# A spectral and gated block with its gradients: inverse rows in a buffer of their own, activation-gradient matmuls dealt between filter chunks and inverse tiles, and the gate applied to w_down

## Chip, cores and metric

The kernel runs on one core of a Trainium2 chip. The metric is the device time in microseconds of one execution, as the median of several runs. Lower is better.

TensorE (PE in the profile, with its weight loads as PEld) does matmuls and writes to PSUM. ScalarE (ACT) and VectorE (DVE) copy results out of PSUM and do the elementwise work. GpSimd (POOL) and SyncE (SP) issue most DMAs; each takes its instructions in order, and so does every engine.

## What is computed

The reference is the forward pass of one block and, with `jax.vjp`, all its gradients. The sequence has S = 2048 positions, the width is D = 576, the hidden width is F = 4608, and everything is bfloat16 on the outside.

```python
def _A_ref(x, w_r, w_i):                       # spectral filter
    X = rfft2(x.astype(float32), axes=(-2, -1)) * (w_r + 1j * w_i)
    return irfft2(X, s=(S, D), axes=(-2, -1)).astype(bfloat16)
def _B_ref(x, w_gate, w_up, w_down):           # bilinear gated unit
    return ((x @ w_gate) * (x @ w_up)) @ w_down
...
sa, ca, ga, sb, cb, gb = split(silu(c) @ w_mod, 6)
h = layernorm(x) * (1 + ca) + sa
x = x + ga * _A_ref(h, w_r, w_i)
h = layernorm(x) * (1 + cb) + sb
x = x + gb * _B_ref(h, w_gate, w_up, w_down)
```

The outputs are the block's output and the gradients with respect to x, w_r, w_i, w_gate, w_up, w_down, c and w_mod, for a given `grad_out`. Two products of `grad_out` matter for this change. The gradient of the hidden activation is `(grad_out * gb) @ w_down.T`. The gradient of `w_down` is `hidden.T @ (grad_out * gb)`.

## The kernel before

The kernel has three parts: a head, a dense part over 36 blocks of 128 hidden columns, and a tail with the backward pass of the spectral filter. The change lies in the head, lines 187 to 477.

The 2048 positions are 16 tiles of 128 (`NT`). The two-dimensional transform is done by matmuls with tables of cosines and sines, in three stages.

- **Row transform** (`s1_norm`, `s1_cols`, `s1_rows`, L280 to L321). For each tile: layer norm and modulation into `hpp`, five transposes (`trp`, copied to `hT`), ten matmuls along the width (`zp`, copied to `zt`), and four along one factor of the sequence (`vp`, copied to `VA`). Statistics are taken for four tiles at once (`norm_stats`).
- **Filter chunks** (`s2_turn`, `s2_filter`, `s2_back`, `s2_inv`, L343 to L385). The 73 groups of four frequencies are handled in 19 chunks. A chunk is transposed from `VA` (`trv`, copied to `VT`), transformed (`xp`, copied to `Xc`), multiplied by the filter on VectorE (`fm`, then `Yg`), transposed back (`try_`, copied to `YT`) and inverse transformed (`ap_`). The last copy puts the result back into `VA`, over the chunk's own input, with the frequency as the outer index: neighbours in the copy's inner loop lie 32 elements apart.
- **Inverse tiles** (`s3_rows`, `s3_cols`, `s3_norm`, L395 to L446). For each tile, six matmuls from `VA` (`upa`, `upb`, copied to `ut`), twelve along the width (`yp`, copied to `yb`), and for each pair of tiles the residual, the second layer norm and its modulation into `h2p`, which a DMA transposes into `h2T`.

Each stage is software pipelined by `pipeline(n, steps)`, which in every round runs the later steps of earlier tiles first.

The six modulation vectors are made by `mod_make(j, wm)` from weights that `mod_load(j)` fetches into one of two `wm` buffers: ten matmuls (`modps`) and two copies to `modh[j]`, then a store to DRAM. The names are MSA, MCA, MGA for the first half and MSB, MCB, MGB for the second; MGB is the gate gb.

Then comes the **activation gradient** (L449 to L477). `grad_out` lies in `gon` and is multiplied in place by MGB, tile by tile (L452). Each tile is transposed on TensorE (L458, 80 matmuls) into `goT`. Blocks of `w_down` are loaded in pairs into `wdn2` and transposed by a DMA into `wdT`. For each of the 36 blocks there are four groups of five 512-column matmuls into `u4p` (L475), each copied out to `ghh_st`, on VectorE for the first nine blocks and on the two engines in turn after that. A finished block is stored to `ghhT_d` in DRAM, from which the dense part reads it. `ghh_st` has two buffers. The scaled `gon` is used again by the dense part, for the gradient of `w_down` (L526).

The program order is not the order on the engines. A planner sorts the instructions by priority, which falls along the program text, and by its own estimate of when each could run, so later instructions may be drawn forward into idle time. `tc.issue_after(i)` puts an instruction behind `i` on its engine, and `tc.high_priority` raises a priority. Once sorted, each engine and each DMA queue runs its list strictly in order, waiting on semaphores.

The dense part begins with matmuls into `gup` (L581). The tail holds the same spectral steps for the gradient. It keeps its inverse result in a buffer `j_A` of its own, laid out by part, row index and frequency (L835, written at L897, read at L924 and L925).

Of the kernel before, what the change touches and what calls it, by code (L numbers as in the profile page):

```python
# [9 lines left out]
FP32 = mybir.dt.float32  # L10
# [72 lines left out]
def build(ctx, tc, A_x, A_w_r, A_w_i, B_w_gate, B_w_up, B_w_down, c_in, w_mod, grad_out,  # L83
# [59 lines left out]
    def norm_stats(xt, pool, nt, name, rstd_out):  # L143

        st = pool.tile([128, nt, 2, nc.vector.BN_STATS_DIM], FP32, name=name + "_st")
        mv = pool.tile([128, nt, nc.vector.BN_AGGR_DIM], FP32, name=name + "_mv")
        for t in range(nt):
            for h in range(2):
                nc.vector.bn_stats(out=st[:, t, h, :], in_=xt[:, t, h * 288:(h + 1) * 288])
            nc.vector.bn_aggr(out=mv[:, t, :], in_=st[:, t, :, :])  # L150
        nc.scalar.activation(out=rstd_out, in_=mv[:, :, 1], func=ACT.Sqrt, bias=eps_t[:], scale=1.0)
        nc.vector.reciprocal(out=rstd_out, in_=rstd_out)
        nmr = pool.tile([128, nt], FP32, name=name + "_nmr")
        nc.vector.scalar_tensor_tensor(out=nmr[:], in0=mv[:, :, 0], scalar=-1.0, in1=rstd_out, op0=MUL, op1=MUL)
        return nmr
# [31 lines left out]
    with ExitStack() as hs:  # L187
# [17 lines left out]
        modh = [hp1.tile([128, D], BF, name="modh%d" % j) for j in range(6)]  # L205
# [9 lines left out]
        c_bf = hp1.tile([128, 5], BF, name="c_bf")  # L215
        nc.vector.memset(c_bf[:], 0.0)
        with nc.allow_non_contiguous_dma(reason="tiny c load"):
            nc.sync.dma_start(c_bf[:, 0:4], c_in[0, 0:512].rearrange("(m q) -> q m", q=128))
            nc.sync.dma_start(c_bf[64:128, 4:5], c_in[0, 512:576].rearrange("(m q) -> q m", q=64))
# [17 lines left out]
        def mod_load(j):  # L237
            wm = hw2.tile([128, 5, D], BF, name="wm")
            nc.sync.dma_start(wm[:, 0:4, :], w_mod[0:512, j * D:(j + 1) * D].rearrange("(m q) n -> q m n", q=128))
            nc.sync.dma_start(wm[:, 4, :], w_mod[448:576, j * D:(j + 1) * D])  # L240
            return wm

        def mod_make(j, wm):
            for h in range(2):
# [5 lines left out]
                else:  # L250
                    evac(modh[j][:, h * 288:(h + 1) * 288], ps[:, 0:288], eng="v")
# [4 lines left out]
        def x_load(c4):  # L256
            xt = hw2.tile([128, 4, D], BF, name="xt", bufs=3)
            nc.sync.dma_start(xt[:], x_v[:, 4 * c4:4 * c4 + 4, :])
            xts.append(xt)

        wms = {MSA: mod_load(MSA)}
        x_load(0)
        wms[MCA] = mod_load(MCA)
        T = {"RD": load_table(hp1, "RD", "tA")}
        T["G1"] = load_table(hp1, "G1", "tB")
        first = mod_make(MSA, wms[MSA])
        mod_make(MCA, wms[MCA])
        with tc.issue_after(first):
# [11 lines left out]
        def s1_norm(t):  # L280
            c4, tt = t // 4, t % 4
            if tt == 0:
# [4 lines left out]
                n1s["nmr"] = norm_stats(xts[c4], hw2, 4, "ln1", rstd1g[:, t:t + 4])  # L287
            n1 = n1s[c4]
            nc.scalar.activation(out=n1[:, tt, :], in_=xts[c4][:, tt, :], func=ACT.Identity, bias=n1s["nmr"][:, tt:tt + 1], scale=rstd1g[:, t:t + 1])
# [12 lines left out]
        def s1_cols(t):  # L302
            zt = zts[t] = hw2.tile([128, 2, FP], BF, name="zt", bufs=3)
            for cc in range(2):
# [3 lines left out]
                evac(zt[:, cc, :], zp[:, :FP], eng=("a" if cc == 0 else "v"))  # L308
            if t == 0:
                with tc.issue_after(mm.ins):  # L310
                    mod_make(MGB, wms[MGB])
# [14 lines left out]
        with tc.issue_after(first):  # L326
            nc.sync.dma_start(wn[:, 0, :, 0:DF], wr_v)
            nc.sync.dma_start(wn[:, 1, :, 0:DF], wi_v)
            for j in (MGA, MSB, MCB):
                wms[j] = mod_load(j)  # L330
        nc.gpsimd.dma_start(wn_d, wn[:].rearrange("k c a f -> k (c a f)"))
        for j in (MGA, MSB, MCB):
            mod_make(j, wms[j])
        r1.close()
        with ExitStack() as rc:
# [15 lines left out]
            def s2_filter(ci):  # L351
# [11 lines left out]
                Yg = Ygs[ci] = c2.tile([128, 4, 128], BF, name="Yg")  # L363
# [13 lines left out]
            def s2_inv(ci):  # L377
# [4 lines left out]
                Ac = VA[:, g0 * 128:(g0 + ng) * 128].rearrange("k (j f e) -> k j e f", f=4, e=2 * NT)  # L382
                evac(Ac, ap_[:, 0:ng, :].rearrange("k j (e f) -> k j e f", f=4), eng="a")

            pipeline(NCH, [s2_turn, s2_filter, s2_back, s2_inv])  # L385
# [6 lines left out]
        Av = VA[:].rearrange("k (f c a) -> k f c a", c=2, a=NT)  # L392
        uts, ybs = {}, {}

        def s3_rows(sa):  # L395
# [3 lines left out]
            for fc in range(3):  # L399
                f0 = FS[fc]  # L400
                o = upa[:, fc, :] if fc < 2 else upb[:, 0, :]
                nc.tensor.matmul(o, lhsT=Av[:, f0:f0 + 128, 0, sa], rhs=T["GB"][:, sa, 1:3, :].rearrange("k v s -> k (v s)"), start=True, stop=False)
                nc.tensor.matmul(o, lhsT=Av[:, f0:f0 + 128, 1, sa], rhs=T["GB"][:, sa, 0:2, :].rearrange("k v s -> k (v s)"), start=False, stop=True)
# [17 lines left out]
        def s3_norm(sa):  # L421
# [14 lines left out]
            for i in range(2):  # L436
# [3 lines left out]
                nc.vector.tensor_tensor(out=h2p[:, s0 + i, 0:D], in0=nm[:], in1=modh[MSB][:], op=ADD)  # L440
# [5 lines left out]
        pipeline(NT, [s3_rows, s3_cols, s3_norm])  # L446


        goT = u4.tile([128, NT, 5, 128], BF, name="goT")  # L449
        for t in range(NT + 1):  # L450
            if t < NT:
                nc.vector.tensor_tensor(out=gon[:, t, :], in0=gon[:, t, :], in1=modh[MGB][:], op=MUL)  # L452
            t -= 1
            if t < 0:
                continue
            pt = u4ps.tile([128, 5, 128], BF, name="u4p")
            for m in range(5):
                nc.tensor.transpose(pt[:, m, :], gonf[:, t * D + m * 128:t * D + (m + 1) * 128], ident[:])  # L458
            evac(goT[:, t, :, :], pt[:])
        FB4 = 2  # L460
        turns = []
        for fb0 in range(0, NFB, FB4):
            wdT = u4w.tile([128, FB4, 5, 128], BF, name="wdT")
            wdn = wdn2[:, (fb0 // FB4) % 2, :, :]
            with tc.issue_after(first):
                nc.sync.dma_start(wdn[:, :, 0:D], B_w_down[fb0 * 128:(fb0 + FB4) * 128, :].rearrange("(j f) d -> f j d", f=128))
# [661 lines left out]
```

## Time and profile before

| quantity | value |
|---|---|
| median of 3 runs | 1629.16 us (1628.55 to 1631.51) |
| the profiled execution's time | 1636.95 us |
| its span, first to last instruction | 1635.2 us |
| TensorE busy | 1566.0 us (96%) |
| VectorE busy | 1007.8 us (62%) |
| ScalarE busy | 567.6 us (35%) |
| mean granted TensorE clock | 0.987 |
| bytes moved by DMA | 280.35 MB |

"Busy" counts an engine as busy while an instruction is in progress. Matmuls overlap in the array, so a TensorE that shows 96% is not at its peak all that time. How many matmuls start in a stretch says more. A row of the groups view gives source line, engine, operation, output and inputs, shapes and count, then busy time and mean duration in ns, then the idle time of the engine just before, with what ended it. An `x` row on line 139 or 141 is a copy out of PSUM by a helper; the tile's name says which one.

### The profile page before, as it was taken

The page shows a single profiled execution, that of the slowest core. Times are in us where ns is not written, and L with a number is a line of the kernel's source. Part 1 is how long each engine was busy: PE and PEld are TensorE (multiplying, and loading weights), DVE is VectorE, ACT ScalarE, POOL GpSimd, SP SyncE. Part 2 cuts the span into 40 slices and gives each one's busy share as a digit, 9 for nine tenths or more (in the row PEclk, how much of TensorE's full clock was granted, in tenths as well). Part 3 has the DMA queues.
Part 4 walks back from the last instruction along what each step waited for, and adds up shares of the span by engine and source line. Part 5 has one row for each costly group of instructions (what it writes and reads, how often), then busy time and mean ns, then how long its engine had stood idle before and what let it go on. Part 6 is the DMA issues. An engine that isn't in the chain of part 4 may idle for free.

```text
span 1635.2 us, 29989 instructions
## 1 busy us (share of the span) xinstructions
PE 1566.0 (96%) x11354; PEld 1066.1 (65%) x11354; DVE 1007.8 (62%) x2642; ACT 567.6 (35%) x1056; POOL 161.3 (10%) x266
## 2 busy tenths in 40 slices
PE   6999999999999999999999999999999879899997
PEld 4645544566767676666767676666766656677765
DVE  7878733566564747565564747565564764678645
ACT  5697522322222222222222222222222355565022
POOL 0101100101000010101010010101000001100232
PEclk9999999999999999999999999999999989999998
DMA  9866976586768586776767686876757786636674
GB/s 349 289 183 196 267 214 192 148 162 123 145 134 165 114 170 121 158 147 114 161 129 153 135 161 117 161 135 142 158 103 136 190 240 202 231 97 193 254 216 151
DMA packets 482242, 280.35 MB, mean 171 GB/s; under 512 B 404753, under 2 KB 449426, under 8 KB 481202
## 3 DMA queue, kind: packets, MB, share of 16 engines
q1 hardware_dynamic: 462098, 204.26, 55.1%
q0 software_dynamic: 20000, 74.19, 15.5%
q8 instruction: 88, 1.44, 0.4%
q14 instruction: 56, 0.46, 0.1%
HBM read 108.51 MB, written 82.31 MB: 117 GB/s over the span
## 4 chain that ended last, share of the span: by engine, by line
PE 74%; DMA 6%; DVE 4%; issue 2%; ACT 2%; SPq 0%; POOL 0%; ACTq 0%; DVEq 0%; POOLq 0%
PE u57p L526 25%; PE gup L581 19%; PE u8p L607 17%; PE u4p L475 6%; PE u3p L1028 3%; DMA Xn<-xn_d 2%; DMA n2c<-n_d 2%; DMA wdB<-in_B_w_down_dram 1%; PE yp L937 1%; DMA out_dram<-o 1%; PE zp L801 1%; DVE gwt L849 0%; ACT u L956 0%; DMA x1t<-x_d 0%; DVE fm L167 0%
## 5 line engine op out<-in xcount | busy, mean ns | idle before, releaser
L612 DVE TENSOR_TENSOR acc<-acc,u8p 128x288 f32<-128x288 f32 x1088 | 429.4, 450 | 352.5 <-PE u8p L607 351.2
L581 PE MATMUL gup<-h2T,wgu 128*128 128x512 bf16 x1440 | 433.1, 379 | 0.0
L607 PE MATMUL u8p<-wT,ggT 128*128 128x288 bf16 x1152 | 314.7, 286 | 4.4 <-DVE acc L612 4.4
L607 PE MATMUL u8p<-wT,guT 128*128 128x288 bf16 x1152 | 314.7, 286 | 0.0
L581 PEld LDWEIGHTS <-wgu 128*128 128x128 bf16 x1440 | 140.8, 98 | 96.7
L528 ACT CAST so<-u57p 128x288 bf16<-128x288 f32 x216 | 86.2, 399 | 326.9 <-PE u57p L526 325.0
L607 PEld LDWEIGHTS <-guT 128*128 128x128 bf16 x1152 | 112.8, 98 | 101.5 <-issue 4.8
L475 PE MATMUL u4p<-goT,wdT 128*128 128x512 bf16 x720 | 165.0, 379 | 1.4 <-ACT ghh_st L139 1.4
L582 ACT CAST gT<-gup 128x512 bf16<-128x512 f32 x144 | 84.4, 586 | 226.6 <-PE gup L581 226.6
L526 PE MATMUL u57p<-gon,hh_sf 128*128 128x288 bf16 x1152 | 150.0, 287 | 0.0
L582 ACT CAST uT<-gup 128x512 bf16<-128x512 f32 x144 | 84.4, 586 | 188.5 <-PE gup L581 186.7
L526 PE MATMUL u57p<-h2p,gu_sf 128*128 128x288 bf16 x1152 | 148.8, 286 | 0.0
L526 PE MATMUL u57p<-h2p,gg_sf 128*128 128x288 bf16 x1152 | 148.2, 286 | 0.0
L1028 PEld LDWEIGHTS <-hl 128*128 128x128 bf16 x1152 | 112.9, 99 | 41.0 <-issue 11.3
L526 PEld LDWEIGHTS <-hh_sf 128*128 128x128 bf16 x1152 | 113.1, 98 | 35.1
L607 PEld LDWEIGHTS <-ggT 128*128 128x128 bf16 x1152 | 112.9, 98 | 29.0
L526 PEld LDWEIGHTS <-gu_sf 128*128 128x128 bf16 x1152 | 112.7, 98 | 28.4
L526 PEld LDWEIGHTS <-gg_sf 128*128 128x128 bf16 x1152 | 112.5, 98 | 28.3
L475 PEld LDWEIGHTS <-wdT 128*128 128x128 bf16 x720 | 69.2, 98 | 74.7 <-issue 1.9
L141 DVE CAST ghh_st<-u4p 128x512 bf16<-128x512 f32 x90 | 61.8, 687 | 67.7 <-PE u4p L475 64.7
L1028 PE MATMUL u3p<-wdB,hl 128*128 128x288 bf16 x672 | 96.4, 291 | 6.6 <-DMA wdB<-in_B_w_down_dram 5.8
L586 POOL DMA_DIRECT2D hhT_d<-hhT x36 | 33.2, 922 | 602.4 <-DVE hhT L583 598.7
(355 smaller groups left out, 1682.6 us busy)
## 6 DMA issues: line engine op xcount, KB each, us to landing
ghhT_d<-ghh_st SPq DMA_DIRECT2D x36, 512.0 KB, 3.3
ghh<-ghhT_d POOLq DMA_DIRECT2D x36, 512.0 KB, 7.7
hhT_d<-hhT POOLq DMA_DIRECT2D x36, 512.0 KB, 6.6
hl<-hhT_d SPq DMA_DIRECT2D x32, 576.0 KB, 7.9
out_dram<-woT SPq DMA_DIRECT2D x72, 128.0 KB, 2.0
wdn<-in_B_w_down_dram SPq DMA_DIRECT2D x18, 288.0 KB, 3.4
out_dram<-so SPq DMA_DIRECT2D x36, 144.0 KB, 2.4
wgu<-in_B_w_up_dram POOLq DMA_DIRECT2D x18, 256.0 KB, 5.3
```

The costliest lines, as they stand in the source:

```text
L141: nc.vector.tensor_copy(dst, src)
L475: nc.tensor.matmul(pt[:], lhsT=wdT[:, j, m, :], rhs=goT[:, 4 * sb4:4 * sb4 + 4, m, :], start=(m == 0), stop=(m == 4))
L526: mm = nc.tensor.matmul(pw[:, 0:288], lhsT=sf[:, t, :], rhs=rhs_n[:, t, h * 288:(h + 1) * 288], start=(t == 0), stop=(t == NT - 1))
L528: nc.scalar.copy(so[:, h * 288:(h + 1) * 288], pw[:, 0:288])
L581: nc.tensor.matmul(pt[:], lhsT=wgu[:, wi_, m, jw * 128:(jw + 1) * 128], rhs=h2T[:, ts_, m, :], start=(m == 0), stop=(m == 4))
L582: nc.scalar.copy(dstT[:, ts_, :], pt[:])
L586: nc.gpsimd.dma_start(hhT_d[:, :, fb, :].rearrange("tp f x -> f tp x"), hhT[:].rearrange("f (tp ti) p -> f tp (ti p)", ti=2))
L607: nc.tensor.matmul(pu[:, 0:288], lhsT=l_, rhs=r_, start=(k == 0), stop=(k == len(mms) - 1))
L612: nc.vector.tensor_tensor(out=dst, in0=dst, in1=pu[:, 0:288], op=ADD)
L801: nc.tensor.matmul(zp[:, :FP], lhsT=gyTs[t][:, m, :], rhs=T["RD"][:, m, cc, :], start=(m == 0), stop=(m == 4))
L937: nc.tensor.matmul(yp[:, 0:288], lhsT=ut[:, fc, cc * 128:(cc + 1) * 128], rhs=T["IR"][:, fc, cc, h * 288:(h + 1) * 288], start=(k == 0), s ...
L1028: mm = nc.tensor.matmul(p2[:, 0:288], lhsT=hls[fb // 9][:, fb % 9, ti * 128:(ti + 1) * 128], rhs=(wdA[:, fb] if fb < 15 else wdB[:, fb - 1 ...
```

## The change

The inverse copy of the filter chunks writes a new buffer `A_h`, laid out as the tail's, and the inverse tiles read their weights from it. The activation-gradient loop becomes a function `u4_group(g)` that does one group of five matmuls. Four groups are issued after the modulation, two in every round of the chunks' pipeline, two after every inverse tile's row matmuls (copied out by ScalarE), and the rest after the tiles. The chunks' pipeline becomes one step longer and `Yg` gets a third buffer.

The gate is applied to the pairs of `w_down` blocks after their load, ahead of the transpose, so `goT` is transposed from the unscaled `gon`; `gon` itself is still scaled, after the last inverse tile's `h2p`. `modh[MGB]` moves to another pool.

At the start, `c` is fetched with a higher priority. The first tile of x is loaded by itself, then MCA's weights, then the other three tiles, then MSA's weights. MCA is made before MSA, whose copies go to ScalarE. The first tile's statistics are taken alone, those of the next three together. MGB is made after the third tile rather than the first, with its copies on ScalarE. In odd tiles both `zt` copies are on ScalarE. MCB's weights are loaded by GpSimd's queue.

```diff
-    def norm_stats(xt, pool, nt, name, rstd_out):
+    def norm_stats(xt, pool, nt, name, rstd_out, room=None):
...
-        modh = [hp1.tile([128, D], BF, name="modh%d" % j) for j in range(6)]
+        modh = [(u4 if j == MGB else hp1).tile([128, D], BF, name="modh%d" % j) for j in range(6)]
...
+        with tc.high_priority(60), nc.allow_non_contiguous_dma(reason="tiny c load"):
+            c_bf = hp1.tile([128, 5], BF, name="c_bf")
...
         def x_load(c4):
             xt = hw2.tile([128, 4, D], BF, name="xt", bufs=3)
-            nc.sync.dma_start(xt[:], x_v[:, 4 * c4:4 * c4 + 4, :])
             xts.append(xt)
-        wms = {MSA: mod_load(MSA)}
+            t0 = 1 if c4 == 0 else 0
+            if t0:
+                nc.sync.dma_start(xt[:, 0:1, :], x_v[:, 0:1, :])
+                wms[MCA] = mod_load(MCA)
+            nc.sync.dma_start(xt[:, t0:4, :], x_v[:, 4 * c4 + t0:4 * c4 + 4, :])
+        wms = {}
         x_load(0)
-        wms[MCA] = mod_load(MCA)
+        wms[MSA] = mod_load(MSA)
...
-        first = mod_make(MSA, wms[MSA])
         mod_make(MCA, wms[MCA])
+        first = mod_make(MSA, wms[MSA], "a")
...
-                n1s["nmr"] = norm_stats(xts[c4], hw2, 4, "ln1", rstd1g[:, t:t + 4])
+            if t == 0 or tt == (1 if c4 == 0 else 0):
+                n = 1 if t == 0 else 4 - tt
+                nmr = norm_stats(xts[c4][:, tt:tt + n, :], hw2, n, "ln1", rstd1g[:, t:t + n], 4)
+                for k in range(n):
+                    n1s["nmr", t + k] = nmr[:, k:k + 1]
...
-                evac(zt[:, cc, :], zp[:, :FP], eng=("a" if cc == 0 else "v"))
-            if t == 0:
+                evac(zt[:, cc, :], zp[:, :FP], eng=("a" if cc == 0 or t % 2 else "v"))
+            if t == 2:
                 with tc.issue_after(mm.ins):
-                    mod_make(MGB, wms[MGB])
+                    mod_make(MGB, wms[MGB], "a")
...
-            for j in (MGA, MSB, MCB):
+            for j in (MGA, MSB):
                 wms[j] = mod_load(j)
         nc.gpsimd.dma_start(wn_d, wn[:].rearrange("k c a f -> k (c a f)"))
+        wms[MCB] = mod_load(MCB, nc.gpsimd)
         for j in (MGA, MSB, MCB):
             mod_make(j, wms[j])
+        goT = u4.tile([128, NT, 5, 128], BF, name="goT")
+        for t in range(NT):
+            pt = u4ps.tile([128, 5, 128], BF, name="u4p")
+            for m in range(5):
+                nc.tensor.transpose(pt[:, m, :], gonf[:, t * D + m * 128:t * D + (m + 1) * 128], ident[:])
+            evac(goT[:, t, :, :], pt[:])
+        FB4 = 2
+        turns, wdTs, sts, u4_done = [], {}, {}, [0]
+        def u4_group(g, eng=None):
+            fb, sb4 = g // 4, g % 4
+            k, j = fb // FB4, fb % FB4
+            if g % (4 * FB4) == 0:
+                wdTs[k] = u4w.tile([128, FB4, 5, 128], BF, name="wdT")
+                wdn = wdn2[:, k % 2, :, :]
+                with tc.issue_after(first):
+                    nc.sync.dma_start(wdn[:, :, 0:D], B_w_down[fb * 128:(fb + FB4) * 128, :].rearrange("(j f) d -> f j d", f=128))
+                nc.vector.tensor_tensor(out=wdn[:, :, 0:D], in0=wdn[:, :, 0:D], in1=modh[MGB][:].unsqueeze(1).to_broadcast([128, FB4, D]), op=MUL)
+                turns.append(nc.sync.dma_start_transpose(out=wdTs[k][:].rearrange("q j m f -> q (j m) f"), in_=wdn.rearrange("f j d -> f (j d)")).ins)
+            if sb4 == 0:
+                sts[fb] = u4w.tile([128, NT, 128], BF, name="ghh_st", bufs=2)
+            pt = u4ps.tile([128, 4, 128], FP32, name="u4p")
+            for m in range(5):
+                nc.tensor.matmul(pt[:], lhsT=wdTs[k][:, j, m, :], rhs=goT[:, 4 * sb4:4 * sb4 + 4, m, :], start=(m == 0), stop=(m == 4))
+            evac(sts[fb][:, 4 * sb4:4 * sb4 + 4, :], pt[:], eng=eng)
+            if sb4 == 3:
+                nc.sync.dma_start(ghhT_d[fb * 128:(fb + 1) * 128, :], sts[fb][:].rearrange("f t p -> f (t p)"))
+        def u4_groups(n, eng=None):
+            for _ in range(n):
+                u4_group(u4_done[0], eng)
+                u4_done[0] += 1
+        u4_groups(4)
         r1.close()
+        A_h = pool("hA", 1).tile([128, 2, NT, FP], BF, name="A_h")
...
-                Yg = Ygs[ci] = c2.tile([128, 4, 128], BF, name="Yg")
+                Yg = Ygs[ci] = c2.tile([128, 4, 128], BF, name="Yg", bufs=3)
...
-                Ac = VA[:, g0 * 128:(g0 + ng) * 128].rearrange("k (j f e) -> k j e f", f=4, e=2 * NT)
+                Ac = A_h[:].rearrange("k c a f -> k (c a) f")[:, :, f0:f0 + w].rearrange("k e (j f) -> k j e f", f=4)
...
-            pipeline(NCH, [s2_turn, s2_filter, s2_back, s2_inv])
+            pipeline(NCH, [s2_turn, s2_filter, lambda ci: u4_groups(2), s2_back, s2_inv])
...
-                nc.tensor.matmul(o, lhsT=Av[:, f0:f0 + 128, 0, sa], rhs=T["GB"][:, sa, 1:3, :].rearrange("k v s -> k (v s)"), start=True, stop=False)
+                nc.tensor.matmul(o, lhsT=A_h[:, 0, sa, f0:f0 + 128], rhs=T["GB"][:, sa, 1:3, :].rearrange("k v s -> k (v s)"), start=True, stop=False)
...
-        pipeline(NT, [s3_rows, s3_cols, s3_norm])
-        goT = u4.tile([128, NT, 5, 128], BF, name="goT")
...
+        pipeline(NT, [lambda sa: (s3_rows(sa), u4_groups(2, "a")), s3_cols, s3_norm])
+        u4_groups(4 * NFB - u4_done[0])
+        with tc.issue_after(h2_made[-1]):
+            for t in range(NT):
                 nc.vector.tensor_tensor(out=gon[:, t, :], in0=gon[:, t, :], in1=modh[MGB][:], op=MUL)
```

The old loop over the pairs of `w_down` blocks (L462 to L477) is removed; its loads, transposes, matmuls, copies and stores are those of `u4_group`, without the scaling.

## The prediction

> **What bounds the kernel now.** I read the whole span first in stretches cut where the head's stages change on TensorE: the row transform ends at 63.7 us, filter chunks run 71.2 to 132.5, inverse tiles 132.5 to 186.5, then activation-gradient matmuls alone (`u4p`, L475) until the first `gup` matmul at 293.5. Columns: stretch, its length, busy time (instructions) of PE, PEld, DVE, ACT and POOL, granted clock, DMA share, GB/s.
>
> ```profile
> 0.00:63.70 63.70, 48.48 (x388) 33.36 (x389) 51.32 (x165) 39.71 (x75) 5.14 (x16) 0.95 0.93 318
> 71.20:132.50 61.30, 56.00 (x461) 30.31 (x459) 48.60 (x131) 57.81 (x56) 5.16 (x9) 1.00 0.64 198
> 132.50:186.50 54.00, 49.96 (x351) 34.09 (x351) 45.90 (x136) 35.84 (x74) 10.81 (x20) 1.00 0.82 230
> 186.50:293.50 107.00, 105.65 (x490) 47.74 (x489) 38.73 (x66) 31.94 (x55) 2.47 (x5) 1.00 0.75 213
> 293.50:1635.20 1341.70, 1299.30 (x9611) 915.69 (x9609) 819.10 (x2139) 399.89 (x794) 137.71 (x216) 0.99 0.69 157
> ```
>
> The chunks are bound by ScalarE (57.81 of 61.30), the tiles by no engine alone, everything from 186.5 by TensorE. The last row matters most: the diff leaves 293.5 onwards alone, so what the head saves is saved whole. The chain of waits confirms it: the 107 us before `gup` are matmuls back to back, broken once by a store that must land before its buffer is refilled.
>
> ```profile
> 189.62 0.61 DVE ghh_st L141
> ...
> 190.29 5.58 DMA ghhT_d<-ghh_st
> ...
> 196.61 8.81 PE u4p L475 x40
> ...
> 206.12 87.57 PE u4p L475 x405
> 293.70 8.63 PE gup L581 x40
> ```
>
> Next, groups of instructions by line: why the chunks wait for ScalarE.
>
> ```profile
> L139 ACT CAST VA<-ap__1175 128x512 bf16<-128x512 f32 x1 | 2.5, 2537 | 0.0
> L139 ACT CAST Xc<-xp 128x512 bf16<-128x512 f32 x18 | 14.3, 792 | 2.5 <-PE xp L355 2.5
> L139 ACT COPY VT<-trv 128x512 bf16<-128x512 bf16 x18 | 12.2, 677 | 2.9 <-PE trv L347 2.9
> L897 ACT CAST j_A<-apt 128x512 bf16<-128x512 f32 (+1 forms) x19 | 11.1, 583 | 0.4 <-PE apt L896 0.4
> ```
>
> The inverse copy into `VA` takes 2.54 us, its siblings of equal size 0.6 to 0.8. `VA` steps 32 elements between neighbours of the inner loop. The backward pass (L897) makes the same copy into the layout that `A_h` will have, in 0.58 us. In the timeline the `VA` copies start at 92.8, 96.0, 99.2, 102.4: 3.2 us a chunk.
>
> **TensorE's work, counted.** A u4 group is five 512-column matmuls and one copy out, 144 groups in all. In the chain, 87.4 us from 206.12 to the first `gup` at 293.5 hold 82 groups (some records are missing), 1.066 us each. The stretch from 186.5 then holds about 99; the tiles, by 62 weight loads of L475, 12.4; the chunks about 32. A chunk's own 16 small matmuls start four in 0.22 us: 0.88 us. A tile's own are 6 row matmuls 0.11 apart and 12 column matmuls in 1.46 (the 12 `yp` last 1.64, less one pipeline tail): 2.1 us. So TensorE is unused for 61.3 - 19 x 0.88 - 32 x 1.066 = 10.5 us in the chunks and 54 - 16 x 2.1 - 12.4 x 1.066 = 7.2 us in the tiles, then about 1.5 us, and 0.9 us at 69 us, where it waits for the MCB weights: 20 us can be won there, by filling holes.
>
> **The change, part by part.**
>
> *Own buffer.* 18 full copies go from 2.54 to 0.58 us: 35 us of ScalarE in a stage of 61. A chunk then needs on ScalarE 0.6 + 0.7 + 0.6, plus one of its two group copies at 0.59: 2.5 us. VectorE: products 0.76, sums 0.49, `YT` 0.41, the other group copy 0.68, a quarter of a w_down scaling 0.2: 2.55. TensorE: 0.88 + 2 x 1.066 = 3.01. TensorE becomes the bound. Weight loads of `VA`, 143 ns, become 98 as at L924; their matmuls already start 0.11 apart, so I count nothing (at most 96 x 0.045 = 4 us if those loads set the pace).
>
> *Groups dealt out.* 4 groups before the chunks, 2 per chunk (38), 2 per tile (32), 70 left. A tile costs 2.1 + 2.13 = 4.23 us of TensorE; ScalarE 0.6 + 0.8 + 0.86 + 0.15 + 2 x 0.59 = 3.6; VectorE (45.9 us busy per 16 tiles, less 8 group copies of 0.67, plus 4 scalings) 2.8. I take 3.15 a chunk and 4.35 a tile, 3 to 5% over the sum, since in-order engines meet imperfectly, and 2.5 us a stage for filling and draining. The ends: exact sums with 1.5 us a stage; or 3.4 and 4.7 if ScalarE's copies queue behind each other.
>
> *Gate scales w_down.* 18 new VectorE products of 128x1152. No row has that form; the 128x576 ones take 0.45 alone and start 0.37 apart, so 0.8 us, 14.4 in all (bounds 0.45 and 0.90). The 16 `gon` products (0.45) leave the row transform, where VectorE is above 9.8 of 10 us from 30 to 60, and follow the last tile, where it is busy 38.73 of 107: nothing on the path. Were that cover gone, the hidden 7.2 us would show at the first `hh_sf` product near 316. The scaling is one more link, load, VectorE, transpose, on a chain of 3.4 + 3.4 us per pair of filter blocks; pairs are needed every 8 groups, 8.5 us, from two buffers. Nothing, unless VectorE waits for the load (a rival below).
>
> *Row transform.* Today the first tile waits for four tiles' statistics (square root at 12.98) and its transposes start at 15.62; the MGB matmuls stand between, so the second transposes come at 22.29. After it both are 2.5 to 2.7 us apart, set by transposes, copy `hT`, column matmuls in turn.
>
> ```profile
> 15.62 0.71 PE L298 MATMUL trp<-ident,hpp 128*128 128x128 bf16 x5 [3.86 <-DVE hpp L293]
> 17.49 2.62 PE L307 MATMUL zp<-T_RD,hT 128*128 128x292 bf16 x10 [1.15 <-ACT hT L139]
> 19.89 2.58 PE L247 MATMUL modps<-wm,sc_rep 128*128 128x288 bf16 x10
> 22.29 0.46 PE L298 MATMUL trp<-ident,hpp 128*128 128x128 bf16 x5
> ```
>
> With `c` issued ahead of the weights (0.5 us), one tile loaded and measured alone, and MCA made first, MSA's evacuation on ScalarE ends near 12.9 and the first transposes start near 13.4: 2.2 us earlier. The second follow at about 17.7, 4.6 earlier. MGB's ten matmuls (1.3 us warm) return after tile 2, half of them in the step's 0.5 us hole: -0.6. Three more small statistics operations (0.5) and eight zt copies moved to ScalarE lie beside this. I take 4 us, between 0 (the row transform is 0.93 full of DMA, and loads behind the first store issue 1 us later) and 7. The Trainium skill, "TensorE: Matmul & The Clock Gate", Part 1, says that an idle window of about 3.4 us halves TensorE's clock. The trace agrees: ten column matmuls take 2.62 us here at a granted 0.77, and 1.42 at 61.40. By that rule the thinner early work could stay slow one step longer and leave 3 us of the 4.
>
> *MCB's load on POOL's queue.* Its buffer is free only once MGA's matmuls are done, as now, but it no longer stands ahead of SP's table loads; on POOL it is behind the `wn_d` store, issued at 40.8. A 256 KB load lands in 5.1 us from POOL and 3.1 from SP in the list of DMA issues, so 2 us later; transposes and the four groups cover it. The Trainium skill, "DMA: Bandwidth & Descriptors", Specifications, gives 1 us against 0.6 for the first byte; by that the delay is 0.4 us.
>
> **Sum.** Row transform ends 63.7 - 4 = 59.7. Modulation 30 x 0.122 = 3.7, 38 transposes 2.1, four groups 4.3, wait 0.7: 10.8. Chunks 19 x 3.15 + 2.5 = 62.4. Tiles 16 x 4.35 + 2.5 = 72.1. Rest 70 x 1.066 + 1 = 75.6. `gup` starts at 280.6 instead of 293.5: 12.9 us less, span 1622.3. That execution took 1636.95 us in all, 7.8 over the runs' median of 1629.16; I take the saving off the median: 1616.
>
> **Rivals.**
>
> (a) *No holes*: 3.01, 4.23, 1.5 us of filling each, and 4 us won early: 6.6 us more, 1609. For: 105.65 of 107 today with nothing beside. Against: chunks and tiles have four stages with latencies.
>
> (b) *Copies bind the tiles*: ScalarE, 3.6 us of work a tile, must take group copies in order with `ut`, for which column matmuls already wait 10 us in all. At 5 us a tile, 10.4 of the gain goes: 1627.
>
> (c) *VectorE stuck on w_down, slower*: today SP bears the wait for that load (SP's waits: us in all, times, longest).
>
> ```profile
> SPq L477 <- DVE ghh_st L141: 28.1, 12, 5.4
> ...
> SPq L467 <- DMA wdn<-in_B_w_down_dram: 8.6, 2, 5.2
> ```
>
> After it, VectorE does, in order, with the chunk's products behind it and TensorE behind them; SP's store of `ghh_st`, which already waits 28.1 us for copies, comes late behind the transpose too. Held 1.2 us in each of 17 pairs, that is 20 us: 1637. It decides from 12.9 / 17 = 0.76 us a pair. Against: 16 of 18 transposes found their load landed.
>
> (d) *It doesn't do what it says*: the order on TensorE comes from a planner that already drew 44 groups forward, and may deal them as before: about 1629 if the copies' time then falls to no one.
>
> **How the numbers follow.** Forecast 0.60, with its own range 1607 to 1624; (a) 0.12, (b) 0.12, (c) 0.13, (d) 0.03. 0.2%, about what a measurement of this kernel can tell from no change, is 3.3 us: faster takes the forecast, (a) and over half of (b), 0.78; the rest of (b) and (d) make 0.08 for no change; slower 0.14. From 1605 to 1631 leaves out (c) and a little below.
>
> **What would show it.** `A_h` copies near 0.6 us; chunks 3.0 to 3.3 us apart with ScalarE no longer full; tiles 4.2 to 4.6 apart; about 70 groups after the last tile; first transposes before 14 us; `gup` near 281. Chunks at 3.5 or more, or VectorE idle before the scaling on a DMA, make it wrong.

## The result, and the profile after

The changed kernel takes 1642.67 us (median of 4 runs, 1641.52 to 1646.16), beside 1629.72 us for the kernel before. The ratio is 1.0082, with a 95% interval of 1.0063 to 1.0101: it is slower by some 13 us, where 13 us less were forecast.

First the stretches of the span, cut at the same events as before: end of the row transform, first chunk, first inverse tile, end of the tiles, first `gup`. Columns as before: stretch, length, busy time of PE, PEld, DVE, ACT and POOL, granted clock, DMA share, GB/s.

```profile
0.00:69.90 69.90, 50.34 (x415) 36.11 (x416) 46.33 (x146) 47.17 (x92) 5.13 (x16) 0.93 0.85 290
69.90:86.10 16.20, 10.35 (x52) 5.57 (x51) 3.95 (x9) 1.58 (x3) 1.31 (x2) 0.79 0.65 227
86.10:145.50 59.40, 58.87 (x488) 35.19 (x487) 42.95 (x119) 39.98 (x75) 0.52 (x1) 1.00 0.59 179
145.50:219.00 73.50, 68.97 (x447) 42.94 (x446) 49.82 (x137) 49.94 (x101) 13.95 (x26) 1.00 0.84 236
219.00:305.60 86.60, 78.66 (x350) 34.70 (x349) 36.80 (x67) 22.47 (x39) 3.96 (x8) 0.94 0.73 210
305.60:1640.80 1335.20, 1296.21 (x9604) 914.88 (x9609) 819.41 (x2139) 399.79 (x794) 137.54 (x216) 0.99 0.70 157
```

Set against the working of the prediction, the row transform ends at 69.9 us instead of 59.7, the modulation stretch lasts 16.2 instead of 10.8, the chunks 59.4 instead of 62.4, the tiles 73.5 instead of 72.1 and the rest 86.6 instead of 75.6. The sum is `gup` at 305.6 instead of 280.6. The chunks are what they were meant to be, with TensorE busy for 58.87 of 59.40. The loss lies in the row transform, the modulation and the rest, and the low clocks (0.93, 0.79, 0.94) stand in just these rows.

The copy that was 2.54 us, from the timeline of the same run (start, length, engine, line, operation):

```profile
93.34 0.60 ACT L139 CAST A_h<-ap__1180 128x512 bf16<-128x512 f32 x1
```

Next the waits: engine and line, what it waited for, us in total, times, longest.

```profile
DVE wdn L360 <- DMA wdn<-in_B_w_down_dram: 41.4, 15, 8.7
...
PE modps L247 <- DMA wm<-in_w_mod_dram: 6.2, 2, 5.8
```

The first line is rival (c), and larger than it was priced: VectorE stands 41.4 us before the scaling of `w_down`, where (c) took 20. The timeline shows where the large ones end on TensorE. The bracket at the end of a line is the idle time before the instruction, and what ended it.

```profile
59.70 0.76 DVE L360 TENSOR_TENSOR wdn<-wdn,modh 128x1152 bf16<-128x1152 bf16 x1 [5.09 <-DMA wdn<-in_B_w_down_dram]
60.89 0.28 PE L326 MATMUL vp<-zt,T_G 128*128 128x292 bf16 x1 [4.22 <-DVE zt L141]
71.64 0.77 POOL L239 DMA_DIRECT2D wm<-in_w_mod_dram  x1 [20.06 <-PE modps L247]
80.79 2.58 PE L247 MATMUL modps<-wm,sc_rep 128*128 128x288 bf16 x10 [5.85 <-DMA wm<-in_w_mod_dram]
227.46 0.76 DVE L360 TENSOR_TENSOR wdn<-wdn,modh 128x1152 bf16<-128x1152 bf16 x1 [8.67 <-DMA wdn<-in_B_w_down_dram]
230.58 4.85 PE L366 MATMUL u4p<-goT,wdT 128*128 128x512 bf16 x11 [7.27 <-DVE ghh_st L141]
```

Three holes. At 55 us VectorE is held for a load, the copies `zt` and `VA` of the last tiles lie behind it in its list, and TensorE waits 4.22 us for `zt`. At 75 us TensorE waits for MCB's weights, which the POOL queue lands 9.10 us after the issue. At 220 us a `w_down` load takes 9.15 us to land, VectorE is held 8.67, and TensorE 7.27. The matmuls behind each hole also run at about half speed: the granted clock is 0.55 from 61.3 to 65.1 us, 0.55 from 80.8 to 86.1 and 0.50 from 230.6 to 235.4. Ten modulation matmuls take 2.58 us where the kernel before took 1.39 for the same ten. The Trainium skill, "TensorE: Matmul & The Clock Gate", Part 1, gives an idle window of about 3.4 us as what halves the clock; the waits of 4.22, 5.85 and 7.27 us agree with it.

In the tiles the waits are small and regular. The chain of waits for one pair of `w_down` blocks (start, length, what); it comes again at 174.94 us:

```profile
156.30 4.31 DMA wdT<-wdn
160.63 3.18 DMA wdn<-in_B_w_down_dram
...
163.91 0.76 DVE wdn L360
```

The load of a pair can only be issued when the transpose before has freed its buffer. The scaling of that load stands next in VectorE's list. But the transpose of that pair is issued much later, at 194.08 us for the load of 160.63, since it waits for `wdT` to come free. So the scaling has some 30 us to spare, and its transpose gains nothing from VectorE's waiting here. From these readings come the theory, a load on the wrong queue and scalings in the wrong place, and its rivals.

### The profile page after: what moved, and what is told of

Its sections match the earlier page's. It is cut to its first block, busy times and chain, and to the rows that moved or that the text cites. A ratio compares the mean times of both kernels' runs of the same rounds, so it can differ in the third digit from the quotient of the medians.

```text
span 1640.8 us, 30002 instructions
## 1 busy us (share of the span) xinstructions
PE 1563.4 (95%) x11347; PEld 1069.4 (65%) x11354; DVE 999.3 (61%) x2616; ACT 560.9 (34%) x1104; POOL 162.4 (10%) x268
## 4 chain that ended last, share of the span: by engine, by line
PE 79%; DMA 10%; DVE 5%; issue 3%; ACT 2%; SPq 1%; POOL 0%; DVEq 0%; ACTq 0%; POOLq 0%
PE u57p L542 25%; PE gup L597 19%; PE u8p L623 17%; PE u4p L366 7%; PE u3p L1044 4%; DMA wdn<-in_B_w_down_dram 2%; DMA n2c<-n_d 2%; DMA wdT<-wdn 2%; DMA Xn<-xn_d 2%; DMA wdB<-in_B_w_down_dram 1%; DMA wm<-in_w_mod_dram 1%; PE zp L817 1%; PE zp L315 1%; PE yp L460 1%; PE yp L953 1%
## 5 line engine op out<-in xcount | busy, mean ns | idle before, releaser
L139 ACT CAST ghh_st<-u4p 128x512 bf16<-128x512 f32 x88 | 51.1, 586 | 81.0 <-PE u4p L366 73.6
```

The lines of the kernel that those rows point to most:

```text
L139: nc.scalar.copy(dst, src)
```

## The experiments

Ratios are to the kernel before, run on the same chip. The rounds ran on several chips, so rows are compared by their ratios.

| kernel | median, us | ratio, 95% interval |
|---|---|---|
| the change | 1642.67 | 1.0082 [1.0063, 1.0101] |
| MCB's load on SP | 1637.80 | 1.0029 [1.0015, 1.0043] |
| gate on `gon` | 1627.97 | 0.9980 [0.9960, 1.0000] |
| both of these | 1617.49 | 0.9917 [0.9893, 0.9940] |
| before, with the new start alone | 1632.32 | 1.0010 [0.9996, 1.0023] |
| before, with the buffer alone | 1635.07 | 1.0033 [1.0016, 1.0051] |
| both, old start | 1617.60 | 0.9924 [0.9903, 0.9945] |
| both, old start, without the buffer | 1628.61 | 0.9991 [0.9974, 1.0007] |
| MCB on SP, scaling on GpSimd | 1630.30 | 0.9999 [0.9985, 1.0012] |
| MCB on SP, loads a pair ahead | 1633.57 | 1.0017 [1.0000, 1.0033] |
| MCB on SP, scaling later in the list | 1624.52 | 0.9968 [0.9952, 0.9983] |
| the same, gate and up loads later | 1616.23 | 0.9902 [0.9884, 0.9920] |
| both, old start, gate and up loads later | 1616.79 | 0.9915 [0.9896, 0.9933] |

### The two suspects, one by one and together

MCB's load back on SP's queue:

```diff
-            for j in (MGA, MSB):
+            for j in (MGA, MSB, MCB):
                 wms[j] = mod_load(j)
...
-        wms[MCB] = mod_load(MCB, nc.gpsimd)
```

> The changed kernel, with MCB's weights loaded by SP's queue again. Theory of holes (the gain is there, and three waits for loads eat it): the 5.85 us in which TensorE waits for this load after the row transform, and the half clock that follows (10 + 8 matmuls at about twice their time, some 2.5 us), shrink to the before kernel's 1 to 2 us, so 5 to 8 us less than the changed kernel: 1635 to 1638. Rival (the dealt-out order costs time whatever is loaded where): the hole moves, within 2 us of the changed kernel's 1642.

The gate on `gon` ahead of its transposes, as before, and no scaling of `w_down`:

```diff
-        for t in range(NT):
+        for t in range(NT + 1):
+            if t < NT:
+                nc.vector.tensor_tensor(out=gon[:, t, :], in0=gon[:, t, :], in1=modh[MGB][:], op=MUL)
...
-                nc.vector.tensor_tensor(out=wdn[:, :, 0:D], in0=wdn[:, :, 0:D], in1=modh[MGB][:].unsqueeze(1).to_broadcast([128, FB4, D]), op=MUL)
...
-        with tc.issue_after(h2_made[-1]):
-            for t in range(NT):
-                nc.vector.tensor_tensor(out=gon[:, t, :], in0=gon[:, t, :], in1=modh[MGB][:], op=MUL)
```

> The changed kernel, with the gate on grad_out again, ahead of its transposes, and no scaling of w_down. Theory of holes: VectorE's 41.4 us of waiting for w_down go, and with them 5 to 6 us at the end of the row transform, about 0.5 us a tile and the 7.3 us of TensorE near 223 with the cold clock behind it (3 us): 16 to 20 us less, 1622 to 1626. Rival (order): VectorE's 16 products of grad_out return to the row transform, which gets no shorter, and the time stays above 1636.

Both edits:

> Both edits: gate on grad_out, MCB's load on SP. Theory of holes: the savings add, 1614 to 1620, which is about what was predicted for the change. Rival (order): above 1630, since filling TensorE more densely was not worth anything.

The first came out 0.5% faster than the change, the second 1.0% (1627.97, 2 us above the range of its theory), both together 1.65%. The two prices add up, as two causes in different places should, and together they leave a kernel faster than the one before: what is left of the change is worth its forecast. In the first, the wait at the modulation shrinks to 1.42 us, and the other suspect is untouched (timeline and waits of that kernel):

```profile
77.74 1.40 PE L247 MATMUL modps<-wm,sc_rep 128*128 128x288 bf16 x10 [1.42 <-DMA wm<-in_w_mod_dram]
```

```profile
DVE wdn L359 <- DMA wdn<-in_B_w_down_dram: 39.1, 15, 5.6
```

Ten matmuls behind a wait of 1.42 us take 1.40 us, at a granted clock of 1.00: no half speed here.

### The start alone

The kernel before with the diff's edits ahead of the row transform's end (loads of `c` and of the first tile, statistics, order of MCA, MSA and MGB, `zt` copies), and nothing behind it.

> The kernel before, with only the start changed (c first, first tile of x alone, MCA before MSA, MGB after the third tile, zt copies of odd tiles on ScalarE). The prediction gave this 4 us: 1625 to 1626. The changed kernel's trace shows the lead gone by the ninth tile (transposes at 41.37 against 41.43), so the second view expects 0 to 1 us: 1628 to 1630.

1632.32, where the kernel before took 1631.66 in the same round, ratio 1.0010: no gain, as the second view has it, though both times lie above its range. And from the other side, the kernel with both edits, given the old start:

> The kernel with gon gated ahead of its transposes and the last modulation load on SyncE's queue (1617.5 us), with the start of the program back as before (one load of all four rows, statistics of four rows at once, the MGB modulation behind the first row, column evictions on both engines). Theory (the new start only moves the first rows, and the statistics and copies of the first eight tiles set the pace behind them, so that its lead is gone by the ninth): 1616 to 1620, the first transposes near 15.6 us instead of 13.75 and the row transform's end within 1 us of the other's. Rival (the start is worth its lead once the stalls behind it are gone): 1621 to 1623.

Its ratio is 0.9924, beside 0.9917 with the new start: no difference that can be told. Its row transform ends at 63.6 us. With the new start and both edits it ends at 65.4, which is 1.8 us later where at most 1 was expected; in the best kernel it ends at 63.7, though there the first transposes start at 13.98 instead of 15.30. A lead at the first tile is not a lead at the last one.

### Is it the scaling, or where it stands?

The theory that VectorE is held in order has a rival: that the scalings themselves, 18 x 0.76 = 13.6 us of VectorE, or transposes that now depend on VectorE, are the cost. Three kernels, all built on the one with MCB's load on SP. The first gives the scalings to GpSimd (`nc.gpsimd.tensor_tensor` in place of `nc.vector.tensor_tensor`).

> The change with the last modulation load on SyncE's queue (1637.8 us) and the 18 scalings of w_down on GpSimd instead of VectorE; the same products. Theory (the loss is that VectorE, which works its list in order, stands 41 us in all before loads that have not landed, while evictions lie behind it): the waits move to GpSimd, whose other work in the head is small, so VectorE's evictions run; a scaling takes longer there (two to four times 0.76 us), the transposes come 1 to 3 us later each, and the time falls to 1620 to 1630. Rival (the loss is that the transposes come late, whichever engine scales): 1637 or more, since each then comes later still.

1630.30, just past the top of the theory's range. The waits moved as expected, from VectorE to GpSimd, and a scaling takes three times as long there (groups of that kernel: line, operation, count, then busy time and mean ns, then the idle time before it):

```profile
L359 POOL TENSOR_TENSOR wdn<-wdn,modh 128x1152 bf16<-128x1152 bf16 x18 | 43.0, 2394 | 129.9 <-DMA wdn<-in_B_w_down_dram 129.8
```

130 us of waiting on GpSimd cost less than 39 us on VectorE. So the waits matter through what stands behind them. But here TensorE also waited once, 9.6 us, for a late transpose, so this run doesn't settle it. The second tries to set the load a whole pair ahead of its scaling (`wdn_turn` is the scaling and the transpose):

```diff
+                if k == 0:
+                    wdn_load(0)
+                    wdn_load(1)
+                    wdn_turn(0)
+                if k + 1 < NFB // FB4:
+                    wdn_turn(k + 1)
+                if k + 2 < NFB // FB4:
+                    wdn_load(k + 2)
```

> The change with the last modulation load on SyncE's queue (1637.8 us), its w_down scaling on VectorE kept, but issued one pair ahead: the scaling and transpose of pair k+1 stand ahead of pair k's groups, and the load of pair k+2 right behind them. The same 18 loads, scalings and transposes in the same two buffers. Theory (VectorE is held because the load of a pair stands directly before its scaling and is issued only when the transpose before has freed the buffer): with a whole pair between load and scaling most of the 39 us of VectorE's waits go, and the time falls to 1617 to 1625, near the kernel that gates gon (1617.5), within 4 us: 18 scalings of 0.76 us cost next to nothing by themselves. Rival (the scaling's own 13.7 us and the transposes behind it on VectorE's order are the cost): 1630 or more, with VectorE's waits for the load shorter than 15 us in all and the time not following.

1633.57, a miss of both. The waits hardly changed (35.7 us in 16), so the kernel tests nothing about their price. It shows why they are there. Its timeline:

```profile
172.11 0.38 SPq L353 DMA_DIRECT2D wdn<-in_B_w_down_dram  x1
...
175.21 0.76 DVE L358 TENSOR_TENSOR wdn<-wdn,modh 128x1152 bf16<-128x1152 bf16 x1 [2.66 <-DMA wdn<-in_B_w_down_dram]
```

The text of the program puts a pair between them, yet the scaling follows its load at once. This fits a planner that sets an instruction where it takes the operand to be ready, and takes the load to land earlier than it does; its own estimates were not read. So the third kernel ties each scaling behind an instruction of VectorE that stands later. `marks` holds such instructions, each with the number of groups issued by then: the sums of the chunks, a copy of each tile, the groups' copies on VectorE.

```diff
+                behind = [i_ for g_, i_ in marks if g_ <= g - 10]
+                with tc.issue_after(behind[-1]) if behind else ExitStack():
+                    nc.vector.tensor_tensor(out=wdn[:, :, 0:D], in0=wdn[:, :, 0:D], in1=modh[MGB][:].unsqueeze(1).to_broadcast([128, FB4, D]), op=MUL)
...
+            marks.append((u4_done[0], evac(ut[:, 2, :], upb[:, 0, :], eng="v")))
```

> The change with the last modulation load on SyncE's queue (1637.8 us), and nothing else moved but the place of 16 of the 18 scalings in VectorE's own list: each is tied behind an instruction of VectorE that stands some ten groups ahead of its pair, so that its load has landed, and well before its transpose is issued. The same loads, scalings and transposes, in the same buffers, on the same engines. Theory (the whole of what is left of the loss is that the planner set each scaling right behind the issue of its load, and VectorE stands there): VectorE's waits for the load, 39.1 us in 15 before, fall below 10, and the time comes to 1617 to 1623, within 5 us of the kernel that gates gon instead (1617.5); the 18 scalings of 0.76 us themselves cost under 5 us. Rival (the scalings' own 13.7 us of VectorE, or the transposes that now wait for VectorE at all, are the cost): 1629 or more with the waits gone.

1624.52, ratio 0.9968: 0.6% better than with MCB on SP alone, but 1.5 us short of the theory's range. First its scalings in the groups of instructions (count, then busy time and mean ns, then idle time before them), then the timeline of SP's queue and TensorE behind the tiles:

```profile
L361 DVE TENSOR_TENSOR wdn<-wdn,modh 128x1152 bf16<-128x1152 bf16 x18 | 13.5, 752 | 0.0
```

```profile
206.73 4.84 SPq L362 DMA_TRANSPOSE wdT<-wdn  x1
211.66 10.77 SPq L490 DMA_TRANSPOSE h2T<-h2p  x1
222.53 0.52 SPq L372 DMA_DIRECT2D ghhT_d<-ghh_st  x1
```

```profile
226.53 8.72 PE L367 MATMUL u4p<-goT,wdT 128*128 128x512 bf16 x26 [12.44 <-ACT ghh_st L139]
```

The idle time before the 18 scalings is 0.0: not one waits for its load, where they waited 39.1 us. The row transform ends at 64.0 us instead of 71.0, the tiles take 67.9 us instead of 74.7, and they end at 199.8, earlier than in any other kernel with the groups dealt out. Ten us of this are then lost in one place, where SP's queue runs a transpose of 10.77 us that took 3.6 for the tiles before it, the store of `ghh_st` stands behind it, and TensorE has no buffer to write to. The wait of 12.44 us is followed by a granted clock of 0.66 (226.5 to 235.3 us).

### What the buffer took

The same hole stands in a kernel without any scaling of `w_down`: the one before, with `A_h` alone.

```diff
+        A_h = pool("hA", 1).tile([128, 2, NT, FP], BF, name="A_h")
...
-                Ac = VA[:, g0 * 128:(g0 + ng) * 128].rearrange("k (j f e) -> k j e f", f=4, e=2 * NT)
+                Ac = A_h[:].rearrange("k c a f -> k (c a) f")[:, :, f0:f0 + w].rearrange("k e (j f) -> k j e f", f=4)
```

> The kernel before, with the inverse rows in their own buffer and nothing else of the change: start, order, gate scaling and loads as before. Theory (the interleaved copy, 2.54 us of ScalarE per chunk, held every fourth or so chunk group in the stage of the filter chunks, and the buffer alone gives that back; the dealing only keeps TensorE fed where the chunks' own chain is not): A_h near 0.6 us a copy, the chunk stage shorter by what ScalarE lay behind, about 4 to 10 us of the 1629: 1620 to 1626. Rival (the buffer is worth nothing without the dealing, since the chunks wait for their DMA turns and products, not for ScalarE): 1628 to 1631.

A miss of both: it came out slower, 1635.07, though its tiles are done 7.6 us earlier than before (the last tile's `yp` starts at 177.4 us instead of 185.1). `gup` starts at 296.1 instead of 293.5. From its timeline, SP's queue and TensorE:

```profile
182.88 1.61 SPq L564 DMA_DIRECT2D wgu<-in_B_w_gate_dram  x1
184.59 7.89 SPq L467 DMA_TRANSPOSE wdT<-wdn  x1
```

```profile
197.61 14.66 PE L475 MATMUL u4p<-goT,wdT 128*128 128x512 bf16 x56 [9.24 <-ACT ghh_st L139]
```

Beside this transpose of 7.89 us (median of the 18: 1.35) run the first gate and up weights of the dense part (`wgu`, L563). In the kernel before they are loaded at 72 us, as soon as the modulation weights are used up. First the kernel before, then the change:

```profile
71.41 0.52 POOL L560 MEMSET wgu<- 64x512 bf16 x1 [17.42 <-PE modps L247]
71.87 0.77 POOL L563 DMA_DIRECT2D wgu<-in_B_w_up_dram  x1
```

```profile
216.87 0.76 POOL L579 DMA_DIRECT2D wgu<-in_B_w_up_dram  x1
```

The memory in which `wgu` waited for its use now holds `A_h`, until the last inverse tile has read it: with `A_h` alone, the last of those reads starts at 176.7 us and the first load of `wgu` at 177.6. The buffer moved more than a megabyte of loads (four of 256 KB and four smaller) from a quiet stretch to the busiest one, without a line of the diff naming them. The kernel without `A_h` shows the other side:

> The kernel that gates gon, with the old start (1617.6 us), without the buffer of its own for the inverse rows: they go back interleaved into VA, at 2.5 us of ScalarE a chunk. So the dealing alone, beside before (1630.4), the buffer alone (1635.1) and both (1617.6). Theory (the two need each other: dealt groups need ScalarE free for their evictions in the chunk stage, and the buffer without the dealing only moves the end of the tiles into a stretch where the transposes of w_down stand behind the gate and up loads): chunks 3.3 to 3.7 us apart instead of 3.05, ScalarE near 0.9 busy in their stage, 1624 to 1632. Rival (the dealing does it all and the buffer is worth under 2 us): 1616 to 1620.

The loads of `wgu` are back at 72.6 us there, and no such hole appears; but ScalarE is full again, and the chunks are 3.36 us apart (60.56 us over 18 steps) instead of 2.88. The window of 75 to 140 us:

```profile
75.00:140.00 65.00, 57.82 (x470) 34.32 (x469) 39.51 (x108) 62.22 (x72) 2.33 (x5) 1.00 0.63 188
```

The buffer alone is +0.33%, the dealing alone -0.09% (no change that can be told), both -0.76%. Neither half, as run, is worth anything by itself: without the buffer ScalarE has no room for the dealt groups' copies, and without the dealing the time won at the end of the tiles is lost in the stretch behind. The buffer alone with its gate and up loads moved out of the way was not run, so it is open whether it would keep its 7.6 us.

Last, the loads moved out of the way in the kernel with the late scalings: they are tied behind later transposes of `w_down`, and all of them go to SP's queue:

```diff
-                        eng = nc.sync if wi_ == 0 else nc.gpsimd
+                        eng = nc.sync if wi_ == 0 or fb < 2 * FBW else nc.gpsimd
+                        with tc.issue_after(turns[(-8, -7, -4, -3)[2 * (fb // FBW) + wi_]]) if fb < 2 * FBW else ExitStack():
```

> The kernel with the 16 scalings set later in VectorE's list (1624.5 us), and the first two sets of gate and up weights, which since the inverse rows have their own buffer are loaded when the last tile's rows are done (196 to 209 us) instead of at 72 to 80 us, are all loaded on SyncE's queue behind the eleventh, twelfth, fifteenth and sixteenth transposes of w_down. Theory (the 12.4 us that TensorE stands after 214 us, at half clock behind it, come from the last transpose of the normed rows, 10.8 us on SyncE's queue beside these loads instead of 3.6, with the store of gradient rows behind it): that transpose takes 3 to 5 us, the hole is gone, the first gate product starts near 281 us instead of 291.0, and the time is 1612 to 1618. Rival (the transpose is slow for another reason, or the loads do as much harm in their new place): 1622 to 1627.

1616.23, ratio 0.9902, within the theory's range. The transpose and the stretches from the first chunk to the first `gup`:

```profile
209.18 3.96 SPq L490 DMA_TRANSPOSE h2T<-h2p  x1
```

```profile
73.80:132.20 58.40, 58.36 (x487) 35.17 (x486) 44.53 (x120) 39.88 (x75) 0.52 (x1) 1.00 0.61 185
132.20:200.10 67.90, 67.90 (x447) 43.47 (x446) 48.53 (x137) 50.87 (x101) 12.95 (x24) 1.00 0.94 257
200.10:281.00 80.90, 76.25 (x352) 34.12 (x350) 37.57 (x69) 22.23 (x39) 2.50 (x5) 1.00 0.83 225
```

The transpose takes 3.96 us, the hole is gone, `gup` starts at 281.0, and TensorE has no gap left in the chunks and the tiles. One `w_down` load, issued at 198.8 us, still takes 9.53 us to land, and now nothing of VectorE waits for it. The move in the kernel that gates `gon`:

> The same move of the gate and up loads in the kernel that gates gon, with the old start (1617.6 us). Theory (its last transpose of the normed rows took 6.8 us instead of 3.1 beside these loads, and VectorE and ScalarE waited some 30 us in all for stores of gradient rows, of which only a part lay on TensorE's path): 1612 to 1616, first gate product at 277 to 280 us instead of 281.3. Rival (that stretch is bound by TensorE's groups, 85.7 of 90 us busy, and the waits are covered): 1616 to 1619.

1616.79 beside 1617.60 in other runs; the intervals of the two ratios overlap, so a gain can't be told, as its rival has it. `gup` starts at 280.5 instead of 281.3: here the loads had cost little, with 6.8 us for the slow transpose instead of 10.8.

The three edits that separate the change from the best kernel give a ladder. `gup` starts at 305.6 us in the change, 297.6 with MCB's load on SP, 291.0 with the scalings set later, 281.0 with the gate and up loads later. The ratios fall from 1.0082 by 0.0053, 0.0061 and 0.0066. These three steps account for the whole loss and for the gain that was forecast. The last one changes the time and, for the up weights, the queue of these loads together; which of the two counts was not run apart.

## Why the prediction was wrong

**Gate scales w_down: "Nothing, unless VectorE waits for the load".** This step failed: VectorE did wait for the load, 41.4 us in 15 waits, where rival (c) took 17 x 1.2 = 20. With MCB's load put right, the kernel still took 1637.80, beside the 1637 of (c). That is in part luck: the waits were twice as long, and only some 18 of the 39.1 us reached the time (ratio 1.0029, against 0.9917 without the scaling). The size of a scaling was right (0.76 us against 0.8), and with the scalings at a better place their cost doesn't show: 1616.23 with them on VectorE, 1616.79 with `gon` gated and none. The price was the place in VectorE's list. The reasoning against the rival, that "16 of 18 transposes found their load landed", says nothing of VectorE. In the kernel before, the loads got their time from other waits of SP: 28.1 us for copies ahead of its stores, and 38.7 us in which 14 of those transposes wait for TensorE to free `wdT`:

```profile
SPq L467 <- PE u4p L475: 38.7, 14, 4.2
```

The scaling stands before that wait and not behind it. A wait that a slow queue hides isn't hidden on the engine to which the change moves it. Nor does the price follow the sum of waits. Those of 1.4 to 2.1 us in the chunks were nearly covered (59.4 us, 58.4 without them); the ones of 5.09, 1.8 to 2.8 (tiles, 73.5 us instead of 67.9) and 8.67 us were not.

**MCB's load on POOL's queue: "2 us later; transposes and the four groups cover it".** Both halves failed. The load takes 9.10 us, not 5.1, and 3.9 us more than on SP's queue (5.2 from the first issue to the matmuls), not 2: the row read was that of a 256 KB load, while `wm` is 576 KB and a second transfer of 144. And the cover was gone. The sum left 38 transposes for this place; the planner had drawn all 80 forward into the row transform. Only eleven group matmuls, 2.5 us, stood between MGA's and MSB's matmuls and MCB's. Moving it back was worth 0.53%.

**Row transform: "I take 4 us".** Worth nothing, the lower end of the range given. The first transposes did start at 13.75 us, as worked out (13.4), but the lead at the first tile is gone by the ninth (41.37 us, 41.43 before). Without scalings that wait, the row transform ends at 63.7 to 65.4 with the new start and at 62.7 to 64.8 with the old. What sets the pace there was not tried: VectorE's statistics and copies, or the DMA engines, whose share is 0.92 of that stretch. The granted 0.77 that the prediction read beside the ten column matmuls is the mean of 10 to 20 us; over those matmuls alone it was 0.50.

**Own buffer.** The copy was right (0.60 us against 0.58), TensorE as the new bound of the chunks too. "I count nothing" was said of the weight loads alone; the place in memory that it takes from the gate and up loads was not in the sum at all, and cost 10 us of `gup` (291.0 against 281.0) where it showed alone.

**Groups dealt out.** Chunks 59.4 us in the change and 58.4 in the best kernel (62.4 forecast); tiles 73.5 and 67.9 (72.1 forecast). Both were a little pessimistic: TensorE's exact sum, 4.23 us a tile, is what the tiles do when nothing is late (67.9 / 16 = 4.24). The rest was too short, 80.9 us instead of 75.6, where TensorE is busy for 76.25 and idle for 4.65. For 4.5 of that it waits for ScalarE's copies; ScalarE and VectorE wait 28.1 us there for stores of `ghh_st` to land.

**What holds.** The diff leaves the last row, from `gup` on, alone. It took 1341.7 us before and 1335.2 in the change; over all profiled runs it lies between 1329.6 and 1341.7, so single executions say less than the medians, and the start of `gup` more. The forecast of 1616 us is what the change does with its three stalls taken out: 1616.23, a ratio of 0.9902 where 0.9919 was forecast. That the sum of the stretches is met, `gup` at 281.0 against 280.6, is in part luck. Row transform and rest come out 4.0 and 5.3 us longer than forecast, modulation, chunks and tiles 0.7, 4.0 and 4.2 shorter. Rival (d), that the planner deals as before, is out: about 70 groups are left behind the last tile, as forecast.

## What to carry to other kernels

When a change puts a computing step between a load and its user, ask where the planner will set that step in the engine's list, and what stands behind it there. The wait that a queue bears for free can become a stall of everything the engine has to do. A new buffer is paid for in what its space was used for: look for the loads that were early because that space was free, and where they will go. Read a transfer's time from a row of its own size on its own queue, and check that the work which is to cover it has not already been drawn forward.

## What was not expected of the hardware

The transposes of the normed rows hold SP's queue for 3.0 to 5.3 us. In four kernels the last of them held it for 6.2 to 10.8 us while the gate and up loads ran beside it. In the same stretch of the change, a `w_down` load of 288 KB took 9.15 us to land instead of 3.3; such a load had also taken 11.35 us in the row transform of the kernel before, beside the modulation weights. In the kernel with the 10.8 us (211.66 to 222.43), the gate and up loads still under way were those of the POOL queue, issued at 207.2 and 208.5 us and landed 14.1 and 13.9 us later. The Trainium skill, "DMA: Bandwidth & Descriptors", Issuing engines are not separate DMA queues, says that all run on the same engines and interleave, and these times agree: another queue was no shelter.

GpSimd takes 2.39 us for the 128x1152 product that VectorE does in 0.76. The interleaved copy of the chunks, at 64 bytes between neighbours, cost ScalarE 2.43 to 2.60 us before, and 0.60 in rows. With the dealt groups beside it, it grew from 2.42 at the first chunk to 2.93 near the last; why was not tried.
